# Attention's products with the probabilities and into the state as single float32 matmuls instead of three float16 ones

## The chip, the cores and the metric

The kernel runs on one core of a Trainium2 chip. The metric is the device time of one execution in microseconds (us), lower is better; runs are compared by their median. The engines are named as in the profile: PE is TensorE (matmul) and PEld its loads of the stationary operand, DVE is VectorE, ACT is ScalarE, POOL is GpSimd, SP is SyncE, which issues most DMAs.

## The reference

Three stages follow each other. An mLSTM attention over 4 batches, 8 heads, 768 tokens and 40 elements a head (a recurrence over tokens, with gates), a dense feed-forward layer of 3072 tokens (320 to 2048 to 320, leaky relu), and a layer of 8 experts (320 to 1024 to 320, relu) of which each token takes one:

```python
    for t in range(S):
        kt, vt, qt = (k[:, :, t], v[:, :, t], q[:, :, t])
        m_new = np.maximum(f_gate[:, :, t] + m, i_gate[:, :, t])
        f_stab = np.exp(f_gate[:, :, t] + m - m_new)
        i_stab = np.exp(i_gate[:, :, t] - m_new)
        m = m_new
        C = f_stab[:, :, None, None] * C + i_stab[:, :, None, None] * np.einsum('bhd,bhe->bhde', vt, kt)
        n = f_stab[:, :, None] * n + i_stab[:, :, None] * kt
        h_tilde = np.einsum('bhde,bhe->bhd', C, qt)
        nq = np.einsum('bhd,bhd->bh', n, qt)[:, :, None]
        denom = np.maximum(np.abs(nq), 1.0)
        y[:, :, t] = o * h_tilde / denom          # o: sigmoid of the output gate
...
    h = x @ w_in
    g = np.maximum(0.01 * h, h)
    return (g @ w_out).astype(np.float32)
...
    for e in range(E):
        mask = e_idx == e                         # e_idx: argmax of x @ w_gate
        h = np.maximum(x[mask] @ w1[e], 0.0)
        out[mask] = gate_w[mask, None] * eom[mask, e, None] * (h @ w2[e])
```

## The kernel before

**Attention** is computed in chunks of 128 tokens. A unit is one batch of one chunk with all 8 heads, so there are 24 units (6 chunks of 4 batches), each the function `unit`. Within a unit the scores are `k` times `q` (PE, line 762), DVE multiplies them by the decay between tokens (`gm`, line 366 as a helper), and the product, called probabilities here, is multiplied with the values, to which a column of ones is appended for the denominator (41 columns; PE, lines 782 to 784). What earlier chunks left comes from a state of 41 x 40 for each head (`o2`, line 799), and `state` (line 845 on) adds the weighted values of a chunk to it, for two batches at a time on two groups of output columns of PE (line 852). There are ten calls of `state`, two for each chunk but the last.

**Numbers.** Where a float32 operand enters a product, it is split into a float16 and a float16 remainder, and the product is three float16 products: high by high, high by low, low by high. The split is a scaled copy on ACT (`copy`, line 375) and a subtraction on DVE (`low`, line 363) or POOL (`less`, line 366). For the probabilities POOL also makes the float16 copy (line 768), but for the units in `PA`, where ACT does.

**Dense** work is 96 steps of two feed-forward tiles for a pair of 128-token tiles: 16 products in `gemm1` (line 903), leaky relu on ACT and DVE, a split by ACT and POOL (`gl`), then 12 products in `gemm2` (lines 925 to 927). The first steps need the attention of units 0 and 1 and the weights, which come as float64, are narrowed by integer operations on DVE and split. Behind the dense steps come the routing and 26 or more blocks of experts (lines 1169 to 1211).

**Order.** Every piece of work has a planned time (`UNITS`, `OFF`, `TICKS`, `WL`, ...). `Order.run` makes a list schedule of all instructions by planned time, with its own costs of operations (a float32 matmul at four times its columns), and writes out the order of each engine's queue. So on every engine an instruction that waits holds up all behind it. Buffers of attention are taken in turn from lists (`Bufs`): `raw_r` holds the loaded queries, keys and values, `QK` the split queries and keys, `GM` the decay and then the probabilities, `PH`/`PL`, `VH`/`VL` and `WVH`/`WVL` the split probabilities, values and weighted values. `S`, the PSUM tile of the scores, has one buffer, used by a unit's two halves of four heads in turn.

Of the kernel before, what the change touches and what calls it, by code (L numbers as in the profile page):

```python
# [25 lines left out]
E = 8  # L26
F = 1024
NTILE = NT // 128
PF = 10                      # pairs of tiles from here on share the dense weights' last pass
TA = 2 * PF                  # token tiles of the first dispatch  # L30
NBA = TA - E + 1             # full blocks that TA tiles always hold
NBH = E // 2                 # first blocks of the rest: up to half a block of two experts each
NBB = NBH + NTILE + E // 2 - 1 - NBA    # blocks of the rest, at most
# [3 lines left out]
S_V = 2.0 ** 5  # L37
S_C = 2.0 ** -4
S_N = 2.0 ** 15
# [25 lines left out]
class Slots:  # L65
    """a tile pool whose tags keep the order of their tiles"""
# [13 lines left out]
class Order:  # L80
    """the order of every engine's instructions: a list schedule by planned time"""
# [61 lines left out]
    def run(self, instrs, planned, pools):  # L143
# [49 lines left out]
        wait = {e: [] for e in self.ENGINES}     # (ready time, i)  # L193
        avail = {e: [] for e in self.ENGINES}    # (priority, i)
# [98 lines left out]
class Bufs:  # L293
    """buffers in turn, each free again once its last reader is out"""
# [12 lines left out]
# the plan: times of the units, of their stages, of the dense steps and of the weights' loads and splits  # L307
UNITS = [2.7, 0, 19, 17.2, 28.8, 32, 42.5, 46.5]
UNITS += [16 + 2.87 * i for i in range(16)]      # from the ninth on in ticks
# [20 lines left out]
# units whose decay between tokens the tensor engine adds up  # L330
PEU = 6
# what the Pool engine takes from the vector engine: packs, reciprocals times gates, gates from these chunks on,
# remainders of queries and keys, of weights
# [5 lines left out]
# units whose weights the scalar engine rounds; whose remainders the vector engine takes  # L339
PA = {3, 4, 6}  # L340
LV = {4}
# weights that the scalar engine scales; units with one transpose for query and key
WA = {(2, 0)}
MT = set()
# where blocks begin that few inputs use
RARE = [26, 28]
# the last planned time of a fixed order; lead and queue of the loads
# [5 lines left out]
def emit(tc, gates, qkv, og, w_in, w_out, w_gate, w1, w2, out):  # L353
# [23 lines left out]
    # arena views  # L377
# [44 lines left out]
    maskb = cp.tile([128, C], BF, name="maskb")      # -1e30 where the key is behind the query  # L422
# [47 lines left out]
    def narrow(r):  # L470
        """float64 words -> float32"""
        n = r.shape[1]
        cv = cv64()
        a, b = (x[:, 0:n] for x in cv)
        lo, hi = r[:, :, 0], r[:, :, 1]
        V.tensor_scalar(out=a, in0=hi, scalar1=3, scalar2=0x3FFFFFF8, op0=ALU.logical_shift_left,
                        op1=ALU.bitwise_and)
        yield 0.35
        stt(V, b, hi, -0x40000000, a, ALU.bitwise_and, ALU.bitwise_or)
        yield 0.65  # L480
        stt(V, a, lo, 29, b, ALU.logical_shift_right, ALU.bitwise_or)
        return a.bitcast(F32), cv

    def piece_win(j, blk, lead):
# [6 lines left out]
        if blk < 2:  # L491
            split(r, win_v[:, j, blk, :], win_v[:, j, 2 + blk, :], S_WIN, helper((j, blk)))
        else:
            # two column blocks' last rows: the remainders of each on the other half of the partitions
            for n in range(2):
                t, h, l = win_v[:, j + n, 4, :], slice(64 * n, 64 * n + 64), slice(64 - 64 * n, 128 - 64 * n)
                copy(t[h], r[h], S_WIN)
                low(t[l], r[h], S_WIN, t[h])
# [25 lines left out]
    def piece_w2(e, k0, n, until=0.0):  # L524
        """until: the time at which what lay there is used"""
# [24 lines left out]
    raw_r = Bufs([R.f32(2 * DM + H * D1) for _ in range(3)], "raw_r")  # L550
    QK = Bufs([R.f16(2, H, 128) for _ in range(4)], "QK")
    QKT = Bufs([R.f16(2 * H, 128) for _ in range(2)], "QKT")
    VH = Bufs([R.f16(H, 42) for _ in range(2)], "VH")
    VL = Bufs([R.f16(H, 42) for _ in range(2)], "VL")
    GM = Bufs([R.f32(H, C) for _ in range(3)], "GM")
    PH = Bufs([R.f16(4, C) for _ in range(4)], "PH")
    PL = Bufs([R.f16(4, C) for _ in range(4)], "PL")
    WV = Bufs([R.f32(H, D1) for _ in range(2)], "WV")
    WVH = Bufs([R.f16(H, 42) for _ in range(3)], "WVH")
    WVL = Bufs([R3.f16(H, 42) for _ in range(3)], "WVL")  # L560
# [26 lines left out]
    def parts(c):  # L587
        """g and b of chunk c as a sum of three bfloat16 parts, one on each group of 32 partitions"""
# [9 lines left out]
    def arguments(c, h0, tag):  # L598
        """g of the query + b of the key, masked, of four heads: [key, head, query]"""
# [15 lines left out]
    def emit_gates(c0, c1):  # L615
        """gates of chunks c0 to c1: g and b by token, decay of the chunk"""
# [33 lines left out]
        outs = [(gw, wT, S_V)]  # L650
# [19 lines left out]
    def emit_sig(c):  # L670
        """output gates of two chunks"""
# [15 lines left out]
    def unit(i):  # L687
        """one (batch, chunk) of all heads"""
# [18 lines left out]
        if i in QG:  # L707
            scaled(G, raw[:, 0:2 * DM], S_QK)
# [12 lines left out]
        else:  # L721
            for a, x in ((qt, qr), (kt, kr)):
                SP.dma_start_transpose(out=a, in_=x.rearrange("p h d -> p (h d)"))
        if i >= PEU:
# [15 lines left out]
        if c < NC - 1:  # L740
            wv, wvh, wvl = WV(), WVH(), WVL()
# [3 lines left out]
            yield 0.7  # L745
            copy(wvh[:, :, 0:D1], wv)
            yield 0.3
            less(True, wvl[:, :, 0:D1], wv, wvh[:, :, 0:D1])
            WV.free(wv)
            st[c, b] = (kr, wvh, wvl, qk)  # L750
        yield to("v")
        vh, vl = VH(), VL()
        copy(vh[:, :, 0:D1], v, S_V)
        low(vl[:, :, 0:D1], v, S_V, vh[:, :, 0:D1])
        raw_r.free(raw)
        pp = []
        for hf in range(2):
# [6 lines left out]
            ph, pl = PH(), PL()  # L764
            if i in PA:
                copy(ph, p32)
            else:
                G.tensor_scalar(out=ph, in0=p32, scalar1=1.0, scalar2=0.0, op0=ALU.mult, op1=ALU.add)
            yield 0.5
            less(not (i in LV), pl, p32, ph)  # L770
            if hf:
                GM.free(gm)
            pp.append((ph, pl))
# [4 lines left out]
        def pv(hf):  # L778
            ph, pl = pp[hf]
            for h in range(4):  # L780
                g = 4 * hf + h
                T.matmul(o1[:, g, :], ph[:, h, :], vh[:, g, 0:D1], start=True, stop=False)
                T.matmul(o1[:, g, :], ph[:, h, :], vl[:, g, 0:D1], start=False, stop=False)
                T.matmul(o1[:, g, :], pl[:, h, :], vh[:, g, 0:D1], start=False, stop=True)

        yield to("p")
        pv(0)
        pv(1)
        PH.free(pp[0][0], pp[1][0])
        PL.free(pp[0][1], pp[1][1])  # L790
        VH.free(vh)
        VL.free(vl)
# [36 lines left out]
        if c == NC - 1:  # L829
            QK.free(qk)  # L830
# [14 lines left out]
    def state(c, pr):  # L845
        up = ps.tile([128, H, D1], F32, tag="aux", name="up", bufs=3)
        for h in range(H):
            for m in range(3):
                for n, o in ((0, 0), (1, 64)):
                    kr, wvh, wvl, _ = st[c, 2 * pr + n]  # L850
                    k0, k1 = ((0, 64), (80, 128), (0, 64))[m] if n == 0 else ((0, 40), (80, 120), (0, 40))[m]
                    T.matmul(up[o:o + k1 - k0, h, :], kr[:, h, k0:k1], (wvh, wvh, wvl)[m][:, h, 0:D1],
                             start=(m == 0), stop=(m == 2))
        for n in range(2):
            QK.free(st[c, 2 * pr + n][3])
            WVH.free(st[c, 2 * pr + n][1])
            WVL.free(st[c, 2 * pr + n][2])
# [37 lines left out]
    def gemm1(xT, n, kp):  # L895
        """two feed-forward tiles: their leaky relu, split"""
# [54 lines left out]
    late = []           # for the logits of the last tiles, behind the first blocks of experts  # L951

# [1 line left out]
    def routing():  # L954
# [21 lines left out]
        half = [rt([128, E], F32, f"half{i}") for i in range(2)]      # block and row of an expert's half  # L976
# [12 lines left out]
        def dispatch(first, bufs, R1, RS, group):  # L989
            """slots of the blocks: their rows, tokens, scales and experts"""  # L990
# [23 lines left out]
            # scale  # L1014
# [9 lines left out]
            # rank in the expert  # L1024
# [22 lines left out]
            # blocks of the experts  # L1047
# [28 lines left out]
            # block of every token, out of the way for those that the other dispatch holds  # L1076
            def of_expert(i, a, r):
                """a of the expert of every token"""
# [8 lines left out]
            if not first:  # L1087
                # behind the full blocks: half a block
# [9 lines left out]
            # slot -> token  # L1098
# [23 lines left out]
            # row c * 512 + b * 128 + p is token b * 768 + c * 128 + p; none beyond the last  # L1122
# [52 lines left out]
        def experts(q):  # L1175
            """rows of the block and their expert: one for all or a fixed one for each half"""
# [42 lines left out]
        def chain(q0, q1, ahead):  # L1219
            """blocks q0 to q1, each one's second product after the next one's first"""  # L1220
# [105 lines left out]
    for j in range(4):  # L1326
        # these lie where the dense weights of steps up to t lay: two pieces of w_in, then w_out
# [76 lines left out]
```

## Time and profile before

| | before |
|---|---|
| median of 3 runs | 726.77 us (726.21 to 727.49) |
| span of the profiled execution | 721.0 us |
| PE busy | 596.5 us (83%), mean granted clock 0.966 |
| DVE busy | 486.8 us (68%) |
| ACT busy | 369.6 us (51%) |
| POOL busy | 391.2 us (54%) |

The span reaches from the first to the last instruction of the one execution that was profiled. That execution has no other time of its own; the median of the runs is 5.8 us above its span. PE's busy time is counted to modelled ends of overlapping matmuls, so distances between starts say more than durations. Shares over the whole span hide that the stages have different limits.

### The profile page before, as it was taken

To read this page: it belongs to the slowest core of one execution; us is meant where nothing else is said; L and a number is where in the kernel's file an instruction comes from. 1 tells how busy PE (TensorE), PEld (TensorE's weight loads), DVE (VectorE), ACT (ScalarE), POOL (GpSimd) and SP (SyncE) were. 2 spreads that over 40 slices of the span, in tenths; PEclk is the share of its full clock that TensorE was granted. 3 is DMA by queue.
4 is the path that set the end of the run, shared out by engine and by line. 5 is a ranking of instruction groups with operands and counts; after the bars stand their busy time and mean duration, and the time that the engine had idled before them with its cause. 6 is when DMAs were issued, how large, how long until landed. Compare 5 with 4: busy or idle time off the path is not lost. (4 is left out here: it accounts for less than half of the span.)

```text
span 721.0 us, 15741 instructions
## 1 busy us (share of the span) xinstructions
PE 596.5 (83%) x5624; PEld 426.0 (59%) x5624; DVE 486.8 (68%) x871; ACT 369.6 (51%) x772; POOL 391.2 (54%) x392
## 2 busy tenths in 40 slices
PE   3447779769787788977898899999699999999894
PEld 1235557547666566756676687776455655665552
DVE  7999999995588789779698876688635722122110
ACT  5546464677665676777655566655332222222220
POOL 6867887466866858867665544524523422223111
PEclk9997999999999999989999999999899999999997
DMA  8686893681957796987666656544599877777632
GB/s 226 228 150 85 184 259 111 209 215 27 186 159 159 211 237 123 228 185 178 136 161 153 170 153 193 155 129 129 165 198 180 160 155 131 159 151 154 148 88 50
DMA packets 215081, 116.77 MB, mean 162 GB/s; under 512 B 170011, under 2 KB 202523, under 8 KB 215004
## 3 DMA queue, kind: packets, MB, share of 16 engines
q1 hardware_dynamic: 212092, 106.68, 64.6%
q0 software_dynamic: 2912, 9.05, 4.5%
q8 instruction: 50, 0.82, 0.5%
q14 instruction: 27, 0.22, 0.1%
HBM read 64.58 MB, written 9.06 MB: 102 GB/s over the span
## 5 line engine op out<-in xcount | busy, mean ns | idle before, releaser
L903 PE MATMUL hp<-xT,arena 128*128 128x256 f16 x1536 | 197.2, 279 | 8.8 <-DVE g L366 7.8
L366 POOL TENSOR_TENSOR gl<-g,gh 128x512 f16<-128x512 f32 x96 | 131.8, 1374 | 111.1 <-ACT gh L375 108.7
L903 PEld LDWEIGHTS <-arena 128*128 128x128 f16 x1536 | 148.3, 100 | 31.5 <-issue 5.7
L925 PE MATMUL acc<-arena,gh 128*128 128x320 f16 x384 | 117.3, 307 | 14.3 <-DVE arena L1276 4.8
L927 PE MATMUL acc<-arena,gl 128*128 128x320 f16 x384 | 117.1, 308 | 9.9 <-POOL gl L366 9.8
L366 POOL TENSOR_TENSOR arena<-arena 128x512 f16<-128x512 f32 (+5 forms) x94 | 111.2, 1195 | 18.5 <-ACT arena L375 10.2
L926 PE MATMUL acc<-arena,gh 128*128 128x320 f16 x384 | 117.4, 306 | 0.5 <-POOL arena L366 0.5
L363 DVE SCALAR_TENSOR_TENSOR r<-hp,r 128x512 f16<-128x512 f32 x52 | 35.9, 691 | 120.8 <-ACT r L1194 106.5
L363 DVE SCALAR_TENSOR_TENSOR arena<-arena 128x328 f16<-128x328 f32 (+7 forms) x113 | 99.1, 888 | 9.3 <-ACT arena L375 7.1
L1188 PE MATMUL hp<-arena,xbb 128*128 (+1 forms) x480 | 95.5, 382 | 5.9 <-issue 5.6
L375 ACT ACTIVATE gh<-g 128x512 f16<-128x512 f32 x96 | 60.1, 626 | 70.3 <-DVE g L366 67.6
L366 DVE TENSOR_TENSOR g<-hp,t 128x512 f32<-128x512 f32 x96 | 65.2, 680 | 41.6 <-ACT t L375 36.0
L1207 PE MATMUL y<-arena,rT 128*128 (+1 forms) x720 | 90.4, 299 | 0.8 <-DMA rT<-r 0.5
L375 ACT ACTIVATE arena<-arena 128x328 f16<-128x328 f32 (+5 forms) x128 | 72.9, 599 | 33.3 <-DVE arena L363 12.7
L1207 PEld LDWEIGHTS <-rT 128*128 128x128 f16 (+1 forms) x720 | 61.8, 101 | 28.0 <-DMA rT<-r 1.4
L1211 POOL DMA_INDIRECT out<-ys,si x26 | 26.8, 1030 | 90.2 <-ACT ys L1210 83.3
L1188 PEld LDWEIGHTS <-xbb 128*128 128x128 f16 (+1 forms) x480 | 41.5, 102 | 53.1 <-issue 10.7
L375 ACT ACTIVATE t<-hp 128x512 f32<-128x512 f32 x96 | 56.1, 585 | 30.0 <-PE hp L903 29.9
L363 DVE SCALAR_TENSOR_TENSOR arena<-stg,arena 128x960 f16<-128x960 f32 (+3 forms) x48 | 57.5, 1198 | 15.3 <-ACT arena L375 14.9
L1194 ACT ACTIVATE r<-hp 128x512 f16<-128x512 f32 x52 | 31.0, 597 | 65.5 <-PE hp L1188 49.3
L375 ACT ACTIVATE arena<-stg 128x1024 f16<-128x1024 f32 (+2 forms) x48 | 46.9, 978 | 17.6 <-DMA stg<-w 10.6
L1169 POOL DMA_INDIRECT xbb<-x2rows,gi x26 | 28.0, 1077 | 49.0 <-PE hp L1188 42.9
(242 smaller groups left out, 855.3 us busy)
## 6 DMA issues: line engine op xcount, KB each, us to landing
stg<-w SPq DMA_DIRECT2D x24, 512.0 KB
arena<-qkv SPq DMA_DIRECT2D x24, 484.0 KB
arena<-gd SPq DMA_DIRECT2D x18, 512.0 KB
stg<-w SPq DMA_DIRECT2D x16, 480.0 KB
raw<-w_in SPq DMA_DIRECT2D x10, 512.0 KB
arena<-w_out SPq DMA_DIRECT2D x8, 640.0 KB
x2rows<-x2r SPq DMA_DIRECT2D x24, 192.0 KB
arena<-og SPq DMA_DIRECT2D x6, 640.0 KB
```

Of the source, the lines that this page charges most:

```text
L363: eng.scalar_tensor_tensor(out=o, in0=a, scalar=s, in1=b, op0=op0, op1=op1)
L366: eng.tensor_tensor(out=o, in0=a, in1=b, op=op)
L375: A.activation(out=o, in_=a, func=AF.Copy, scale=s)
L903: T.matmul(hp[:, kk, :], win_v[:, j, wb, o:o + 128], xT[:, xb, :], start=(m == 0), stop=(m == 7))
L925: T.matmul(acc[i], gh[:, kk, r], wh, start=(k == lo), stop=False)
L926: T.matmul(acc[i], gh[:, kk, r], wl, start=False, stop=False)
L927: T.matmul(acc[i], gl[:, kk, r], wh, start=False, stop=(k == hi))
L1169: G.indirect_dma_start(out=xb, out_offset=None, in_=rows, in_offset=bass.IndirectOffsetOnAxis(ap=gi[:, i:i + 1], axis=0), bounds_check=(TA ...
L1188: T.matmul(hp[n][r], xT[:, xb, r], W1v[:, e, wb, n * 512:(n + 1) * 512].rearrange("p a b -> p (a b)"), start=(m == 0), stop=(m == 7))
L1194: A.activation(out=r[:, 0, :], in_=hp[n], func=AF.Relu)
L1207: T.matmul(y[r], a[:, r], W2v[:, e, k, m, :].rearrange("p a b -> p (a b)"), start=(k + n == 0), stop=(k == 7 and n == 2))
L1211: G.indirect_dma_start(out=out, out_offset=bass.IndirectOffsetOnAxis(ap=D_[s][1][:, i:i + 1], axis=0), in_=ys, in_offset=None, bounds_chec ...
```

## The change

The products of probabilities and values, and those of keys and weighted values into the state, take the float32 operands as they are: one float32 matmul in place of three float16 ones. The splits of probabilities, values and weighted values go, with their buffers. In their place there are more buffers for what is now held longer: six of `raw_r` (the state reads keys from it, so it is freed only there), four of `GM` and of `WV`, and two instead of four of `QK`, freed behind the transposes. Where POOL scales queries and keys, it writes to a buffer of its own (`QKS`) and no longer in place, since the state needs the unscaled keys. The constants of scale follow. The plan's times are unchanged. Comments, which the change also removes, are left out here:

```diff
-S_V = 2.0 ** 5
-S_C = 2.0 ** -4
-S_N = 2.0 ** 15
+S_W = 2.0 ** 5
+S_C = 2.0
+S_N = S_QK * S_QK
...
-PA = {3, 4, 6}
-LV = {4}
...
-    raw_r = Bufs([R.f32(2 * DM + H * D1) for _ in range(3)], "raw_r")
-    QK = Bufs([R.f16(2, H, 128) for _ in range(4)], "QK")
+    raw_r = Bufs([R.f32(2 * DM + H * D1) for _ in range(6)], "raw_r")
+    QKS = R.f32(2 * DM)
+    QK = Bufs([R.f16(2, H, 128) for _ in range(2)], "QK")
     QKT = Bufs([R.f16(2 * H, 128) for _ in range(2)], "QKT")
-    VH = Bufs([R.f16(H, 42) for _ in range(2)], "VH")
-    VL = Bufs([R.f16(H, 42) for _ in range(2)], "VL")
-    GM = Bufs([R.f32(H, C) for _ in range(3)], "GM")
-    PH = Bufs([R.f16(4, C) for _ in range(4)], "PH")
-    PL = Bufs([R.f16(4, C) for _ in range(4)], "PL")
-    WV = Bufs([R.f32(H, D1) for _ in range(2)], "WV")
-    WVH = Bufs([R.f16(H, 42) for _ in range(3)], "WVH")
-    WVL = Bufs([R3.f16(H, 42) for _ in range(3)], "WVL")
+    GM = Bufs([R.f32(H, C) for _ in range(4)], "GM")
+    WV = Bufs([R.f32(H, D1) for _ in range(4)], "WV")
...
         if i in QG:
-            scaled(G, raw[:, 0:2 * DM], S_QK)
+            G.tensor_scalar(out=QKS, in0=raw[:, 0:2 * DM], scalar1=S_QK, scalar2=0.0, op0=ALU.mult, op1=ALU.add)
+            q, k = (QKS[:, u * DM:(u + 1) * DM].rearrange("p (h d) -> p h d", h=H) for u in range(2))
...
             for a, x in ((qt, qr), (kt, kr)):
                 SP.dma_start_transpose(out=a, in_=x.rearrange("p h d -> p (h d)"))
+        QK.free(qk)
...
         if c < NC - 1:
-            wv, wvh, wvl = WV(), WVH(), WVL()
+            wv = WV()
             w = wT[:, c, b * H:(b + 1) * H].unsqueeze(2)
             tt(G, wv, v, w.to_broadcast([128, H, D1]), ALU.mult)
-            yield 0.7
-            copy(wvh[:, :, 0:D1], wv)
-            yield 0.3
-            less(True, wvl[:, :, 0:D1], wv, wvh[:, :, 0:D1])
-            WV.free(wv)
-            st[c, b] = (kr, wvh, wvl, qk)
-        yield to("v")
-        vh, vl = VH(), VL()
-        copy(vh[:, :, 0:D1], v, S_V)
-        low(vl[:, :, 0:D1], v, S_V, vh[:, :, 0:D1])
-        raw_r.free(raw)
-        pp = []
+            st[c, b] = (raw, wv)
         for hf in range(2):
...
             tt(V, p32, sc, p32, ALU.mult)
-            ph, pl = PH(), PL()
-            if i in PA:
-                copy(ph, p32)
-            else:
-                G.tensor_scalar(out=ph, in0=p32, scalar1=1.0, scalar2=0.0, op0=ALU.mult, op1=ALU.add)
-            yield 0.5
-            less(not (i in LV), pl, p32, ph)
-            if hf:
-                GM.free(gm)
-            pp.append((ph, pl))
...
-        def pv(hf):
-            ph, pl = pp[hf]
-            for h in range(4):
-                g = 4 * hf + h
-                T.matmul(o1[:, g, :], ph[:, h, :], vh[:, g, 0:D1], start=True, stop=False)
-                T.matmul(o1[:, g, :], ph[:, h, :], vl[:, g, 0:D1], start=False, stop=False)
-                T.matmul(o1[:, g, :], pl[:, h, :], vh[:, g, 0:D1], start=False, stop=True)
-
         yield to("p")
-        pv(0)
-        pv(1)
...
+        for h in range(H):
+            T.matmul(o1[:, h, :], gm[:, h, :], v[:, h, :], start=True, stop=True)
+        GM.free(gm)
+        if c == NC - 1:
+            raw_r.free(raw)
...
         for h in range(H):
-            for m in range(3):
-                for n, o in ((0, 0), (1, 64)):
-                    kr, wvh, wvl, _ = st[c, 2 * pr + n]
-                    k0, k1 = ((0, 64), (80, 128), (0, 64))[m] if n == 0 else ((0, 40), (80, 120), (0, 40))[m]
-                    T.matmul(up[o:o + k1 - k0, h, :], kr[:, h, k0:k1], (wvh, wvh, wvl)[m][:, h, 0:D1],
-                             start=(m == 0), stop=(m == 2))
+            for n, o in ((0, 0), (1, 64)):
+                raw, wv = st[c, 2 * pr + n]
+                k0 = DM + h * D
+                T.matmul(up[o:o + 64 - 24 * n, h, :], raw[:, k0:k0 + 64 - 24 * n], wv[:, h, :], start=True, stop=True)
         for n in range(2):
-            QK.free(st[c, 2 * pr + n][3])
-            WVH.free(st[c, 2 * pr + n][1])
-            WVL.free(st[c, 2 * pr + n][2])
+            raw_r.free(st[c, 2 * pr + n][0])
+            WV.free(st[c, 2 * pr + n][1])
```

## Rows read from the trace of the kernel before

**Rows 1.** Busy time by stage: stretch, length, busy us (instructions) of each engine, clock.

```profile
0.00:48.00 48.00, 18.60 (x165) 11.04 (x166) 43.04 (x69) 27.54 (x54) 35.22 (x65) 1.00 0.81 215
48.00:160.00 112.00, 84.67 (x900) 63.82 (x901) 107.34 (x159) 63.20 (x135) 79.25 (x68) 0.92 0.74 173
160.00:410.00 250.00, 208.60 (x2414) 164.88 (x2414) 199.17 (x330) 167.63 (x386) 173.90 (x164) 0.97 0.70 164
410.00:510.00 100.00, 96.79 (x851) 76.74 (x850) 74.59 (x140) 59.36 (x101) 42.70 (x36) 1.00 0.54 153
```

(The engines are PE, PEld, DVE, ACT and POOL in this order; behind the clock stand the share of DMA and GB/s.)

**Rows 2.** Timeline of PE, two dense steps: start us, length, line, operands, count.

```profile
446.56 1.91 PE L903 MATMUL hp<-xT,arena 128*128 128x256 f16 x16
449.94 1.91 PE L903 MATMUL hp<-xT,arena 128*128 128x256 f16 x16
```

**Rows 3.** PE's waits from 160 to 410 us: total us, times, longest.

```profile
PE sc L762 <- DVE arena L366: 16.4, 10, 4.0
...
PE o L784 <- POOL arena L366: 6.0, 7, 1.8
PE acc L925 <- DVE arena L1276: 3.9, 1, 3.9
PE acc L925 <- DVE arena L366: 3.8, 3, 1.9
PE hp L903 <- DVE g L366: 2.4, 1, 2.4
PE o L782 <- POOL arena L768: 1.7, 3, 0.6
```

**Rows 4.** Groups of instructions on POOL, whole span: count, busy us, mean ns.

```profile
L366 POOL TENSOR_TENSOR arena<-arena 128x512 f16<-128x512 f32 x48 | 63.9, 1337 | 2.7 <-ACT arena L375 1.1
L768 POOL TENSOR_SCALAR arena<-arena 128x512 f16<-128x512 f32 x42 | 30.4, 724 | 15.3 <-DVE arena L366 14.5 <-DVE rd L366 0.7
...
L366 POOL TENSOR_TENSOR arena<-arena 128x328 f16<-128x328 f32 x20 | 20.2, 1017 | 6.0 <-ACT arena L375 5.8
```

**Rows 5.** The same on DVE, from 0 to 160 us.

```profile
L363 DVE SCALAR_TENSOR_TENSOR arena<-arena 128x328 f16<-128x328 f32 x9 | 7.0, 776 | 0.2
...
L366 DVE TENSOR_TENSOR arena<-arena 128x512 f16<-128x512 f32 x2 | 1.5, 734 | 0.0
```

**Rows 6.** The same on DVE, whole span: one operation with its input elsewhere.

```profile
L363 DVE SCALAR_TENSOR_TENSOR x2r<-arena,x2r 128x256 f16<-128x256 f32 x20 | 14.5, 725 | 0.7 <-ACT x2r L375 0.6
...
L363 DVE SCALAR_TENSOR_TENSOR x2r<-acc,x2r 128x256 f16<-128x256 f32 x4 | 1.7, 417 | 0.4 <-ACT x2r L375 0.4
```

(`arena` lies in SBUF, `acc` in PSUM.)

**Rows 7.** Busy time of line 363 alone: stretch, length, DVE us, clock, DMA.

```profile
0.00:160.00 160.00, 83.78 (x99) 0.95 0.76 185
160.00:410.00 250.00, 107.35 (x136) 0.97 0.70 164
```

**Rows 8.** Timeline of PE: first and last of twelve value products in a row.

```profile
69.12 0.18 PE L784 MATMUL o<-arena 128*128 128x41 f16 x1
...
69.40 0.18 PE L783 MATMUL o<-arena 128*128 128x41 f16 x1
```

**Rows 9.** Timeline of PE: float32 transposes and the product behind them.

```profile
67.47 0.43 PE L661 MATMUL pt<-ident,arena 32*128 32x32 f32 x4
67.83 0.31 PE L927 MATMUL acc<-arena,gl 128*128 128x320 f16 x1
```

**Rows 10.** Weight loads, float32 and float16: least, median and greatest ns.

```profile
L661 PEld LDWEIGHTS pt<-ident,arena x16: 133/138/219, 7.2 to 70.5; 32*128 32x128 f32 x16
...
L782 PEld LDWEIGHTS <-arena x192: 95/96/152, 21.7 to 405.4; 128*128 128x128 f16 x192
```

**Rows 11.** Timeline of PE: one state of 48 products and what follows.

```profile
240.59 0.89 PE L852 MATMUL up<-arena 128*64 128x41 f16 x48
241.40 0.28 PE L903 MATMUL hp<-xT,arena 128*128 128x256 f16 x1
```

**Rows 12.** Busy time of line 782 alone (a third of the value products).

```profile
160.00:410.00 250.00, 12.55 (x128) 10.54 (x128) 0.97 0.70 164
```

More of the change, by code (lines that the diff above doesn't have):

```diff
@@ L649, in emit_gates @@
         yield GW
-        outs = [(gw, wT, S_V)]
+        outs = [(gw, wT, S_W)]
         if c0:
@@ L776, in unit @@
         o1 = ps.tile([128, H, D1], F32, tag="aux", name="o1", bufs=3)
-        def pv(hf):
-            ph, pl = pp[hf]
-            for h in range(4):
-                g = 4 * hf + h
-                T.matmul(o1[:, g, :], ph[:, h, :], vh[:, g, 0:D1], start=True, stop=False)
-                T.matmul(o1[:, g, :], ph[:, h, :], vl[:, g, 0:D1], start=False, stop=False)
-                T.matmul(o1[:, g, :], pl[:, h, :], vh[:, g, 0:D1], start=False, stop=True)
-        yield to("p")
-        pv(0)
-        pv(1)
[L789 to L792, printed above, removed]
+        yield to("p")
+        for h in range(H):
[3 more added lines that the diff above has]
+            raw_r.free(raw)
         yield to("c")
@@ L828, in unit @@
         SP.dma_start_transpose(out=xTs[i // 2][:, :, j * 128:(j + 1) * 128], in_=xr)
-        if c == NC - 1:
-            QK.free(qk)
         if c < NC - 1 and b % 2:
```

## Prediction

> **What bounds the kernel now.** I read the busy table by stage first [rows 1]. Up to 48 us there are only the first attention units, the gates and the conversion of the weights; the dense steps start there. Up to 160 us VectorE (DVE) is busy 43.0 of 48 us and then 107.3 of 112 us, so it is the bound; TensorE (PE) has 27 us of idle time in the second of these stretches. From 160 to 410 us nothing is full: PE 208.6 of 250 us, DVE 199.2, GpSimd (POOL) 173.9, ScalarE (ACT) 167.6. From 410 to 510 us, with attention over, PE is busy 96.8 of 100 us. What follows (some 211 us of expert blocks) holds no line that the change touches. Dense steps at full pace follow each other by 3.38 us [rows 2]; 96 of them are 324 us of the 462 us between 48 and 510, and the rest is attention's own PE work and PE idle time. So the end moves by PE's idle time and PE's work up to 510 us, whichever engine causes it. In the third stretch I read who ends PE's idle time [rows 3]: the scores wait for DVE 16.4 us (one PSUM buffer for both halves of a unit, so the second half's scores wait until DVE has multiplied the first), the dense products wait for DVE 3.9, 3.8 and 2.4 us, and the value products wait for POOL, which splits the probabilities, 6.0 and 1.7 us. This gives 26.5 us behind DVE's queue and 7.7 us behind the split itself; most of what is left of the idle time waits on a transpose by DMA that nothing here touches.
>
> **What is taken away.** Off POOL go the rounding of probabilities (42 x 724 ns = 30.4 us), their remainders (46 of the 48 of that shape, the other two split weights: 46 x 1.337 = 61.5 us) and the remainders of weighted values (20.2 us), 112 us in all [rows 4]. Off ACT go 44 copies of 328 elements and six of 512. Off DVE go 24 remainders of values; nine of them, 7.0 us, lie before 160 us, and the two of probabilities, 1.5 us, too [rows 5]. The value products' wait for POOL is gone; next in line for them is DVE's multiply of the second half, which ends before the split did, so I count the 7.7 us as gained.
>
> **What a lighter POOL gives DVE.** The same remainder of 256 elements takes 725 ns with both operands in SBUF and 417 ns with one in PSUM [rows 6]: 42% of the former is lost to something that the latter doesn't meet, and POOL, busy for most of both stretches, is the other engine that works on SBUF in this way. Remainders and other such operations of that line are 83.8 us of DVE before 160 us and 107.4 us from 160 to 410 [rows 7]. Before 160 us: 83.8 - 7.0 = 76.8 us, 42% of it 32 us. POOL is busy 35.2 + 79.3 = 114.5 us there [rows 1] and loses the work of units 0 to 7, 10 x 0.724 + 14 x 1.337 + 8 x 1.017 = 34 us, 30%. So the gain lies between 0 and 32 x 0.30 = 9.6 us; nothing shows which of the two engines' operations overlap, and I take the middle, 5 us.
>
> **The stretch before 160 us.** DVE sets its length, so it shortens by 7.0 + 1.5 + 5 = 13.5 us (ends: 8.5 and 18.1; below the lower end only if DMA, at 0.74 to 0.81 of its engines' time [rows 1], comes to bind).
>
> **The stretch from 160 to 410 us.** DVE loses 15 remainders, some 12 us at the mean of [rows 5], and by the same reckoning between 0 and 18 us of contention: (107.4 - 12) x 0.42 = 40 us, of which POOL loses (32 x 0.724 + 32 x 1.337 + 12 x 1.017) / 173.9 = 45%. With the middle, 9 us, its busy share falls from 199/250 = 0.80 to 178/250 = 0.71. Time spent behind a queue goes about as u/(1 - u), 3.9 before and 2.5 after, so 37% of the 26.5 us goes: 9.8 us (ends: 0 and 26.5). With the 7.7 us this is 17.5 us of PE idle time.
>
> **What is added: float32 products.** No row of before shows one. 24 f16 products of a unit start about 25.5 ns apart [rows 8], 0.61 us a unit. Now there are 8 in float32. The nearest rows are float32 transposes with 128 stationary columns, on 32 partitions and moving only 32 columns: four take 0.43 us with the last one's length of 0.222, so they start 69 ns apart, and the next f16 product starts 0.36 us after the first, 90 ns for each [rows 9]. Their weight loads last 138 ns by the median, f16's of 128 columns 96 [rows 10]. Lower end: 70 ns, a transpose's price. Upper end: 4 x 69 = 276 ns, if each float32 product costs four such passes with their loads. I take the geometric middle, 140 ns. The state is now 16 float32 products in place of 48 f16 ones, which took 240.59 to 241.40 us, 17 ns each, since two column groups run side by side [rows 11]; I keep that ratio of 17/25.5 for float32. With x us for a product, units 8 to 23 (16 of them: 128 products of each kind after 160 us, 8 a unit [rows 12]) and the six states of chunks 2 to 4 add 16 (8x - 0.61) + 6 (16 * 0.667x - 0.81) = 192x - 14.7 us: at 140 ns 12.2 us; at 70 ns -1.3; at 276 ns 38.3. I count all of it, since PE becomes the bound of this stretch. For units 0 to 7 it is 8 * 0.51 + 4 * 0.68 = 6.8 us and hides in PE's 27 us of idle time before 160 us; without that cover it would be on the path too.
>
> The float32 weight load is where pages speak against this change. The Trainium skill, page "TensorE: Matmul & The Clock Gate", section "Weight-path perf modes", says that the fast weight load is off for FP32; the 138 ns against 96 [rows 10] agree in direction. The page "FP8 and Floating Point Precision", section "TensorE Precision Notes", says that true FP32 makes four passes through the array; no row here shows one. With four passes at the f16 row's 25.5 ns, an estimate from that page, x would be 102 ns and the sum 7.3 us lower than mine; with four passes that each reload at 69 ns it would be the upper end.
>
> **What I cost at nothing.** The scaled queries and keys go to one separate buffer (eight units): the same operation on POOL, and its wait for the unit before, whose readers are ACT's two copies and POOL's own remainders, is covered by the distance between units, 250/16 = 15.6 us after 160 us. If that cover fails, gates and weighted values queue behind it on POOL, about a microsecond each. QK falls from four to two buffers, but is free after the transposes rather than after the state; if they are late, ACT's copy of the unit after next waits, and dense copies behind it. Inputs are held until the state, in six buffers instead of three: if one isn't free, the load waits on SP's queue, and the transposes and weight loads behind it. The gate buffers are four now for a longer hold. All are in proportion to the longer or shorter holds.
>
> **Sum.** Before 160 us -13.5; after -17.5 + 12.2 = -5.3; together -18.8 us. The profiled span is 721.0 us, the median of the runs 726.77, so 5.8 us lie around the span. 721.0 - 18.8 + 5.8 = 708 us.
>
> **Rivals.**
> - *Float32 is dear* (the other side). PE pays 276 ns a product; the relief is the same 13.5 + 17.5 = 31 us, the price 38.3: +7.3, 734 us. The change loses from 192x - 14.7 = 31, x = 238 ns. For it: PE is 83% busy in that stretch, and the loads of float32 are slower in the rows. Against it: the transposes' 69 to 90 ns. By itself: the page on precision, with its four passes, is the rule that would make it so.
> - *Float32 is cheap.* 70 ns: -31 - 1.3, 694 us. For it: the transposes' spacing; against it: they move fewer columns and only pass on what they read.
> - *The relief is not passed on.* The order on each engine is written out, so a freed POOL or DVE may only wait elsewhere: no gain from contention or from DVE's queue. -8.5 - 7.7 + 12.2 = -4.0, 723 us. For it: after 160 us no engine is full; against it: the waits of [rows 3] are short and many, behind a queue.
> - *The buffers bind*, or an order that the planner writes anew stalls somewhere: of unknown size, both signs, 10 us or so.
>
> **How the numbers follow.** About the forecast (700 to 717) 0.42; cheap float32 or more relief (below 700) 0.20; relief not passed on (717 to 729) 0.20; dear float32 (above) 0.15; buffers and order 0.03. Within 0.2% of 726.8, about what a measurement of this kernel can tell from no change, is 725.3 to 728.2. Faster: 0.42 + 0.20 + most of the third, 0.13 = 0.75; slower 0.18; same 0.07. The range from 688 to 733 leaves out the deep end of the second case and most of the fourth.
>
> **What would show it.** Right: 108 instructions fewer on POOL, 26 on DVE, 50 on ACT, 704 on PE; value products that start about 140 ns apart; DVE's SBUF remainders well below 725 ns; scores waiting less for DVE; the dense steps ending near 490 us instead of 510 and the same 211 us after it. Wrong: value products at 240 ns or more; DVE's operations no shorter; a new wait on inputs or on the two QK buffers at ACT or SP; or the DVE-bound stretch no shorter than 150 us.

## The result, and the profile after

The changed kernel takes 703.36 us (median of 4 runs, 700.39 to 704.15), the kernel before 727.13 us in the same comparison (4 runs): a ratio of 0.966, with a 95% interval from 0.9636 to 0.9684. The prediction was 708 us. The execution that was profiled took 700.39 us, its span is 698.6 us. Of the kernels further down, one execution in four with doubled products and four in ten with POOL's work back lay more than 1.5% above the fastest of the same kernel; medians are of the others.

Busy time and instructions of the changed kernel's whole span:

```profile
span 698.6 us, 14850 instructions
PE 620.8 (89%) x5272; PEld 461.1 (66%) x5272; DVE 435.7 (62%) x845; ACT 350.5 (50%) x722; POOL 275.4 (39%) x282
```

POOL lost 115.8 us, DVE 51.1, ACT 19.1, and PE gained 24.3. By stage, with the columns of [rows 1]:

```profile
0.00:48.00 48.00, 28.08 (x163) 20.12 (x164) 35.75 (x70) 24.70 (x46) 21.48 (x51) 1.00 0.81 214
48.00:160.00 112.00, 96.53 (x854) 78.03 (x852) 94.66 (x151) 65.59 (x137) 63.34 (x52) 0.91 0.71 181
160.00:410.00 250.00, 234.49 (x2310) 193.89 (x2308) 180.01 (x328) 161.10 (x362) 100.31 (x93) 0.98 0.73 173
410.00:510.00 100.00, 87.41 (x714) 65.86 (x713) 71.03 (x145) 53.43 (x95) 38.06 (x33) 0.97 0.58 153
```

From 160 to 410 us PE is now busy 234.5 of 250 us, where it was 208.6; DVE is no longer full in the first two stretches (35.8 of 48 and 94.7 of 112 us). PE has become the bound behind 160 us. Its waits there, to be read beside [rows 3]:

```profile
PE lp L908 <- DMA x2T<-x2r: 7.2, 8, 2.3
PE sc L745 <- DVE arena L363: 6.5, 6, 2.0
PE lp L908 <- DVE rd L363: 1.4, 1, 1.4
PE acc L887 <- POOL gl L363: 0.3, 1, 0.3
```

The value products wait for nobody any more (7.7 us before), the dense products no longer for DVE (10.1 us before), the scores 6.5 us in place of 16.4. Where the time went is seen in the products of `gemm1` (first start to last start, us), line 903 before and 863 after:

```profile
L903 PE MATMUL hp<-xT,arena x1536: 269/273/422, 48.7 to 510.4; 128*128 128x256 f16 x192
```

```profile
L863 PE MATMUL hp<-xT,arena x1536: 269/273/421, 43.4 to 491.3; 128*128 128x256 f16 x192
```

The dense steps start 5.3 us and end 19.1 us earlier; from that end on it is 207.3 us where it was 210.6.

The new products, grouped (those of probabilities and values, then the state's, for each of its two groups of columns) and on PE's timeline:

```profile
L753 PE MATMUL o<-arena 128*128 128x41 f32 x384 | 52.7, 300 | 0.0
...
L814 PE MATMUL up<-arena 128*64 128x41 f32 x160 | 13.1, 247 | 0.0
L814 PE MATMUL up<-arena 128*40 128x41 f32 x160 | 11.3, 227 | 0.0
```

```profile
200.20 1.13 PE L814 MATMUL up<-arena 128*64 128x41 f32 x32
201.25 1.92 PE L863 MATMUL hp<-xT,arena 128*128 128x256 f16 x16
...
204.64 1.88 PE L753 MATMUL o<-arena 128*128 128x41 f32 x16
206.34 0.37 PE L763 MATMUL o<-arena 120*128 120x41 f16 x8
```

There are 384 instructions for 192 products and 320 for 160: each float32 product is two passes, with a weight load each. A unit's 16 passes take 1.70 us to the start of what follows, 106 ns a pass, 212 ns a product, where three f16 products took 0.61 us a unit [rows 8]; the state's 32 passes take 1.05 us, 66 ns a product, where f16 took 0.81 [rows 11].

### The profile page after: what moved, and what is told of

It reads as the page before. It is cut to its first block, busy times and chain, and to the rows that moved or that the text cites. A ratio compares the mean times of both kernels' runs of the same rounds, so it can differ in the third digit from the quotient of the medians.

```text
span 698.6 us, 14850 instructions
## 1 busy us (share of the span) xinstructions
PE 620.8 (89%) x5272; PEld 461.1 (66%) x5272; DVE 435.7 (62%) x845; ACT 350.5 (50%) x722; POOL 275.4 (39%) x282
## 5 line engine op out<-in xcount | busy, mean ns | idle before, releaser
L363 POOL TENSOR_TENSOR gl<-g,gh 128x512 f16<-128x512 f32 x96 | 125.4, 1307 | 198.2 <-ACT gh L372 186.5
L863 PE MATMUL hp<-xT,arena 128*128 128x256 f16 x1536 | 191.6, 277 | 9.7 <-DVE g L363 5.9
L887 PE MATMUL acc<-arena,gl 128*128 128x320 f16 x384 | 115.5, 305 | 6.1 <-POOL gl L363 6.1
L360 DVE SCALAR_TENSOR_TENSOR arena<-arena 128x320 f16<-128x320 f32 (+6 forms) x89 | 69.1, 785 | 12.3 <-ACT arena L372 11.8
L372 ACT ACTIVATE arena<-arena 128x640 f16<-128x640 f32 (+3 forms) x78 | 50.9, 672 | 26.2 <-DVE arena L360 7.6
L1171 POOL DMA_INDIRECT out<-ys,si x26 | 26.5, 1018 | 88.3 <-ACT ys L1170 80.5
L730 ACT ACTIVATE arena<-arena,bT 128x128 f32<-128x128 f32 x144 | 48.2, 389 | 9.5 <-POOL arena L719 9.4
L753 PE MATMUL o<-arena 128*128 128x41 f32 x384 | 52.7, 300 | 0.0
```

The source lines that it names most:

```text
L360: eng.scalar_tensor_tensor(out=o, in0=a, scalar=s, in1=b, op0=op0, op1=op1)
L363: eng.tensor_tensor(out=o, in0=a, in1=b, op=op)
L372: A.activation(out=o, in_=a, func=AF.Copy, scale=s)
L730: A.activation(out=gm[:, 4 * hf + h, :], in_=gm[:, 4 * hf + h, :], func=AF.Exp, bias=bT[:, c, g:g + 1])
L753: T.matmul(o1[:, h, :], gm[:, h, :], v[:, h, :], start=True, stop=True)
L863: T.matmul(hp[:, kk, :], win_v[:, j, wb, o:o + 128], xT[:, xb, :], start=(m == 0), stop=(m == 7))
```

## The experiments

Theory A is that of the prediction: lifting the splits off POOL, DVE and ACT frees PE from waiting, and PE pays the price of float32 in full where it has become the bound. Rival B: what counted was the products' own wait for the split, and PE hides the price. Rival C came up on the way: the time is a matter of the order that the planner happens to write.

Ratios below are to the kernel before on the same chip, with 95% intervals; differences in us are between medians, to the 703.4 us of the changed kernel unless said otherwise.

**The price on PE, doubled.**

```diff
         for h in range(H):
-            T.matmul(o1[:, h, :], gm[:, h, :], v[:, h, :], start=True, stop=True)
+            for _ in range(2):
+                T.matmul(o1[:, h, :], gm[:, h, :], v[:, h, :], start=True, stop=True)
```

> The changed kernel, but each of the 8 float32 products of probabilities and values is issued twice (the second overwrites the first with the same numbers), so PE gets a second 1.70 us a unit, 41 us in all, and no other engine anything. Theory A (PE is the bound after 150 us, so its price is paid in full there): 16 of 24 units pay, +27 us, and up to 8 us more from the first eight: 728 to 738 us. Rival B (PE still has idle time in which products hide; what the change won was the wait for the split itself): at most half of the 41 us shows, 710 to 720 us.

Measured: 754.2 us, ratio 1.0333 (1.0258 to 1.0408), 51 us more. B is out, and more came than even the 41 us of extra work. Where the rest lies is shown by the timeline of two units' doubled products and by the busy time of the stage:

```profile
203.20 3.66 PE L754 MATMUL o<-arena 128*128 128x41 f32 x32
206.69 1.48 PE L864 MATMUL hp<-xT,arena 128*128 128x256 f16 x12
...
236.73 5.87 PE L754 MATMUL o<-arena 128*128 128x41 f32 x32
242.40 0.48 PE L764 MATMUL o<-arena 120*128 120x41 f16 x8
```

```profile
160.00:410.00 250.00, 237.56 (x2198) 198.50 (x2198) 147.91 (x283) 144.63 (x330) 89.22 (x84) 0.92 0.62 145
```

The granted clock is 0.92 in this stage (mean of 2.4 GHz and stretches at 1.2), 0.98 without the doubling. The same products take 3.5 us at 203 and 5.7 us at 237 us, and from 240 to 280 us the clock is 0.81. Of the first eight units, whose price the prediction had as hidden, the first two take 6.8 us each in place of 3.5, and the dense steps start at 48.1 us in place of 43.4: there it isn't hidden either. These passes take some 212 ns each, with the products doubled as without, twice the 106 ns of later ones; the rows show a granted clock of 1.00 up to 48 us, so they don't say why.

**The price on PE, taken away.**

```diff
+    def top(a):
+        return a.bitcast(BF).rearrange("p (d w) -> p d w", w=2)[:, :, 1]
...
-            T.matmul(o1[:, h, :], gm[:, h, :], v[:, h, :], start=True, stop=True)
+            T.matmul(o1[:, h, :], top(gm[:, h, :]), top(v[:, h, :]), start=True, stop=True)
```

> The changed kernel, but the products of probabilities and values read only the upper 16 bits of each float32 number, as one bfloat16 product: no engine but PE does anything else, the numbers are coarser (left out: the lower 16 bits). PE loses about 1.70 - 0.2 = 1.5 us a unit if the pitch of 25.5 ns of a float16 product holds. Theory A: 16 x 1.5 = 24 us less, 675 to 683 us. Rival B: PE's price is hidden, 693 to 703 us.

Measured: 685.2 us, ratio 0.9436 (0.9369 to 0.9502), 18 us less; A said 20 to 28, B 0 to 10. The eight products of a unit take 0.20 us to the next start, as the expectation had it:

```profile
199.44 0.36 PE L756 MATMUL o<-arena 128*128 128x41 bf16 x8
199.64 0.36 PE L766 MATMUL o<-arena 120*128 120x41 f16 x8
```

So most of the price that PE pays for float32 here is in the end time. At the head it is hidden: the dense steps start at 44.3 us here, no earlier than the 43.4 us of the changed kernel. For this kernel, as for the other variants, the planner writes the order anew; what that alone is worth comes further down.

**The work of the split back on POOL, for nobody.** The results go to a scratch tile (`DH`, `DW`) and the float32 products stay.

```diff
+PA = {3, 4, 6}
+LV = {4}
...
+    DH, DV, DW = R3.f16(4, C), R3.f16(H, 42)[:, :, 0:D1], R3.f16(H, 42)[:, :, 0:D1]
+    for t in (DH, DV, DW):
+        G.memset(t, 0.0)
...
             tt(G, wv, v, w.to_broadcast([128, H, D1]), ALU.mult)
+            yield 0.7
+            pass
+            yield 0.3
+            less(True, DW, wv, DW)
...
             tt(V, p32, sc, p32, ALU.mult)
+            ph = pl = DH
+            if i not in PA:
+                G.tensor_scalar(out=ph, in0=p32, scalar1=1.0, scalar2=0.0, op0=ALU.mult, op1=ALU.add)
+            yield 0.5
+            if i not in LV:
+                less(True, pl, p32, ph)
```

> The changed kernel, but POOL again does its work of the split (42 copies and 46 differences of 512 elements, 20 differences of 328, about 112 us) into a scratch tile that nobody reads: no product waits for it. Theory A (a lighter POOL relieves DVE and POOL's own queue): DVE's difference x2r<-arena of 256 elements goes back from 606 towards 725 ns, and the time rises by 10 to 20 us, 714 to 724 us. Rival B (only the products' own wait for the split counted): at most +5 us, 703 to 708 us, with x2r at about 606 ns.

Measured: 714.7 us, ratio 0.9847 (0.9799 to 0.9895), 11 us more: within A's range, near its lower end, and above B's. Busy time (of an execution of 722.6 us):

```profile
PE 625.5 (87%) x5272; PEld 461.7 (64%) x5272; DVE 470.9 (65%) x845; ACT 350.3 (49%) x722; POOL 395.4 (55%) x393
```

DVE has the same 845 instructions as the changed kernel and takes 470.9 us for them instead of 435.7: 120 us of POOL's work cost DVE 35 us. The one row that I had named as a sign, the difference of 256 elements, went from 606 only to 662 ns; it turned out to wander between 525 and 716 ns from one order to the next in kernels whose DVE and POOL do the same work, so it says nothing, and DVE's total does.

PE's waits from 160 to 410 us, to be read beside [rows 3]:

```profile
PE lp L923 <- DMA x2T<-x2r: 13.8, 11, 2.2
PE sc L754 <- DVE arena L365: 6.1, 4, 2.3
PE hp L878 <- DVE g L365: 1.2, 1, 1.2
PE acc L900 <- DVE arena L1260: 0.8, 1, 0.8
```

Behind DVE's queue PE waits 8.1 us, hardly more than the 6.5 us of the changed kernel and far from the 26.5 us of before, although DVE is busy 192.6 of the 250 us here (199.2 before, 180.0 in the changed kernel).

**The work of the split back on all three engines.** As before, and also ACT's copies, DVE's remainders of the values (`low(DV, v, 32.0, DV)`) and the two of probabilities, all into scratch.

> The changed kernel, but POOL, DVE and ACT all do their work of the split again, into scratch that nobody reads; the products stay float32 and wait for none of it. Theory A: the kernel before, less the products' wait for the split (7.7 us) and plus the price of float32 on PE (18.9 us after 150 us), so 733 to 743 us, slower than before. Rival B: 705 to 712 us.

Measured: 738.4 us, ratio 1.0131 (1.0077 to 1.0186): 35 us above the changed kernel, and slower than before, as A said.

```profile
PE 634.1 (86%) x5272; PEld 465.9 (63%) x5272; DVE 485.1 (66%) x871; ACT 369.1 (50%) x772; POOL 390.0 (53%) x393
```

The engines but PE are busy as before (DVE 486.8, ACT 369.6, POOL 391.2 us there). Without the splits' removal the change is a loss, and since this kernel has all buffers of the changed one, those alone bring no gain. From before to this kernel two things differ by design: PE pays for float32, 16 x (1.70 - 0.61) + 6 x (1.05 - 0.81) = 18.9 us behind 160 us, and the value products no longer wait for the split, 7.7 us [rows 3]. That makes +11.2 us; measured are +11.6 (the interval is 5.6 to 13.5). That the two agree so closely is luck: the order is new too, each scratch tile is one buffer where the splits had two to four, and PE's waits behind DVE's queue from 160 to 410 us are 16.4 us here, not the 26.5 us of before.

**What sets the price of a pass.** Two sets of products with fewer columns in front of the real ones; the results are overwritten.

```diff
         for h in range(H):
+            T.matmul(o1[:, h, 0:20], gm[:, h, :], v[:, h, 0:20], start=True, stop=True)
+        for h in range(H):
+            T.matmul(o1[0:64, h, :], gm[:, h, 0:64], v[:, h, :], start=True, stop=True)
+        for h in range(H):
             T.matmul(o1[:, h, :], gm[:, h, :], v[:, h, :], start=True, stop=True)
```

> The changed kernel with two further sets of 8 float32 products in front of the real ones of each unit, whose results are overwritten: one moves 20 columns in place of 41, one holds 64 stationary columns in place of 128. If loading the stationary operand sets the price of 106 ns a pass, the first set keeps 106 ns and the second falls to about 66 ns or less (the state's passes of 64 and 40 columns start 33 ns apart, two groups side by side). If the moved columns set it, the first set falls to about 52 ns and the second keeps 106 ns. The whole time is of no interest here (some 45 to 60 us above the changed kernel).

```profile
252.34 1.86 PE L753 MATMUL o<-arena 128*128 128x20 f32 x16
254.13 1.13 PE L755 MATMUL o<-arena 128*64 128x41 f32 x16
255.19 2.48 PE L757 MATMUL o<-arena 128*128 128x41 f32 x16
```

With 20 moved columns 16 passes take 1.79 us to the next start, no less than 41 columns take (1.70). With 64 stationary columns they take 1.06 us, 66 ns a pass. So at these sizes the stationary operand sets the price, and with 128 stationary columns the count of moved ones doesn't. It isn't the columns of the load alone: the float32 transposes of before also hold 128, on 32 partitions, and start 69 to 90 ns apart [rows 9]; what makes that difference no run shows. The kernel took 790.9 us in its one execution, 88 us above the changed kernel where 45 to 60 were expected; its granted clock was 0.931 over the span. The Trainium skill, page "TensorE: Matmul & The Clock Gate", section "LDWEIGHTS (loading the stationary operand)", gives the time of a load in nanoseconds as the columns divided by 1.2. Estimated from that, 128 columns are 106.7 ns and 64 columns 53 ns: the distance of passes agrees for 128 (106) and not for 64 (66).

**Half of the change.** Float32 for the probabilities only; the state's three f16 products come back, with their copies and differences, `raw_r` at 4 and `QK` at 4 buffers.

> Half of the change: the products of probabilities and values are float32, those into the state are the three float16 ones again, with ACT's copy and POOL's difference of the weighted values (20 each, 9.3 and 20.2 us), and the buffers that go with it (four of inputs, four of QK). Theory A: POOL's share of the gain in proportion, 20.2/112 of the 19.6 us of all POOL work, 3.5 us, 1 us for ACT, less 2 us that PE saves: 704 to 709 us. Rival (the buffers of the change, held to the state, cost something, or the state's part is where the gain lies): below 700 or above 712 us.

Measured: 710.0 us, ratio 0.976 (0.9708 to 0.9813). It is 6.6 us above the changed kernel and just outside what A gave, which took POOL's whole work at 19.6 us (by the run above it is 11 us). By what the next two runs show, this doesn't tell the two halves apart: the difference is no larger than what order alone makes. Since 710.0 us is 14 us or more below every order of before (see below), it does show that the larger part of the gain needs only the probabilities, and not the buffers held until the state.

**Order alone.** The planner's cost of every float32 instruction on PE, and the planned distance of the dense steps; no instruction is added or taken away.

```diff
-            n *= 4 if mybir.dt.size(q.ins[0].bass_ap.dtype) == 4 else 1
+            n *= 12 if mybir.dt.size(q.ins[0].bass_ap.dtype) == 4 else 1
```

```diff
-TICK = 3.38
+TICK = 3.36
```

> The changed kernel, but its planner takes a float32 product of 41 columns for 205 ns, about what it takes on the chip (212 ns), in place of 68 ns; the instructions are the same, only their order on the engines is written anew. Theory A: nothing in sight depends on it, within 4 us of the changed kernel, 699 to 707 us. Rival C (the gain is a matter of a lucky order): 10 us or more away.

> The changed kernel with the planned distance of dense steps at 3.36 in place of 3.38: no work changes, only the order that the planner writes. It shows how much of any difference between two kernels here is a matter of order. Theory A: within 4 us, 699 to 707 us. Rival C: 10 us or more away.

Measured: with the higher price in the planner 721.2 us (ratio 0.9919, 0.9892 to 0.9946), with 3.36 713.5 us (0.9802, 0.976 to 0.9844). Rival C is right at least so far: order alone is worth 10 to 18 us here. The higher price is right only for the products with the values (205 ns, 212 measured): a product of the state gets 205 ns too, where it takes 66, and a transpose of 32 columns 160 ns, where it takes 69 to 90 [rows 9]. With it, PE's idle time from 40 to 500 us is this:

```profile
PE lp L908 <- DMA x2T<-x2r: 16.4, 13, 3.6
PE sc L745 <- DVE arena L363: 13.4, 5, 4.2
PE hp L863 <- DMA xT<-xr: 8.1, 2, 5.5
```

In the changed kernel the first two are 8.9 and 8.1 us, and the third doesn't occur among its waits. DVE, ACT and POOL are hardly busier or less (425.2, 352.0 and 276.7 us). So I asked how much of the 24 us is order.

**Orders of before, and more of after.** `TICK` at 3.36 and 3.40 in the kernel before, at 3.40 and 3.34 in the changed one.

> The kernel before with the planned distance of dense steps at 3.36 in place of 3.38: no work changes, only the written order. The changed kernel moved from 703 to 714 us by the same edit, so order is worth some 10 us there. Theory A (the change is worth 20 us or so, whatever the order): 720 to 738 us, above all orders of the changed kernel. Rival C (much of the difference is a lucky order of the changed kernel, or an unlucky one of before): 705 to 715 us.

> The kernel before with 3.40: a third order of the same work. Theory A: 720 to 738 us. Rival C: 705 to 715 us.

> The changed kernel with 3.40. Theory A: 700 to 716 us, the mean of its orders some 18 us below that of before. Rival C: 715 to 725 us.

> The changed kernel with 3.34. Theory A: 700 to 716 us. Rival C: 715 to 725 us.

| TICK | before, us | changed, us | ratio of changed |
|---|---|---|---|
| 3.34 | | 705.2 | 0.9721 (0.9682 to 0.9759) |
| 3.36 | 724.4 | 713.5 | 0.9802 (0.976 to 0.9844) |
| 3.38 (as given) | 726.5 | 703.4 | 0.966 (0.9636 to 0.9684) |
| 3.40 | 725.2 | 711.7 | 0.9795 (0.9751 to 0.9839) |
| mean | 725.4 | 708.5 | |

(Ratios are each from the run's own comparison; 3.34 was not run for the kernel before.) The orders of before lie within 2 us of each other, those of the changed kernel within 10 (18 with the other price). Every order of the changed kernel is below every order of before. The change is worth about 17 us by these means (14 with the 721.2 us among its orders), and the order that it happened to get another 5. Against the mean of 708.5 us, the runs above read +46 (products doubled), -23 (products cheap), +6 (POOL's work back) and +30 (all work back); the first, second and last are outside all orders seen, that of POOL alone is not, so its 6 to 11 us may be order, while DVE's 35 us are not: DVE's busy time lies between 425 and 436 us in all five orders of the changed kernel.

No version tried here that does the whole work is faster than the changed kernel as it stands.

## Why the prediction held, step by step

- **The sum** was 708 us: 5 us above the kernel as given, and within 1 us of the mean of its four orders. That is better than its terms deserve: the price of float32 was 7 us too low, the gain before 160 us 6 us too high and the relief behind it 8.5 us too low, and that they nearly cancel is luck. Of the 19.1 us by which the dense steps end earlier some 4 us are in none of these terms, nor are the 3.3 us behind the dense steps, where the prediction had no change.
- **The price of float32** was the geometric middle, 140 ns; it is 212 ns for probabilities and values and 66 instead of 93 ns for the state. Behind 160 us it is 18.9 us in place of 12.2. The step that failed is the choice of a middle between a transpose's 70 ns and four times 69: [rows 9] are one pass, and a product here is two passes of 106 ns, each of them dearer than a transpose (the loads last 192 ns by the median, those of the transposes 138). The doubled instructions show in the counts: PE lost 352 instructions, not the 704 that I named; those of DVE and ACT fell by 26 and 50, as said, POOL's by 110 (108 said).
- **That PE pays in full behind 160 us** holds, within what order leaves open, by the runs with doubled and cheap products (+46 to +51 us for 41 us of work, -18 to -23 where 24 were due). **That the first eight units hide theirs** failed in the doubled run: the first two stand at the head of everything, and their passes take twice as long as later ones. In the changed kernel this is covered: the dense steps start 5.3 us earlier than before, and no earlier still with the cheap products.
- **The relief behind 160 us** was mis-sized low: 7.7 us for the wait on the split and 37% of 26.5 us behind DVE's queue. The first went entirely, of the second 20.0 us are gone (26.5 to 6.5). PE's idle time fell from 41.4 to 15.5 us, 26 us where I had 17.5. The share by u/(1 - u) was not only too timid: with POOL's work back DVE's busy share is 0.77, which by that rule leaves 23 of the 26.5 us, and PE waits 8.1 us. So, as far as this one order shows, this part of the gain did not come by a lighter POOL making DVE less busy; with all three engines' work back the wait is 16.4 us. Which of the removed operations, or how much of order, shortened it stays open.
- **The contention between POOL and DVE** was the right mechanism, and of line 363 about the right size. The same line (360 after), to be read beside [rows 7]:

```profile
0.00:160.00 160.00, 69.35 (x92) 0.94 0.74 191
160.00:410.00 250.00, 85.30 (x125) 0.98 0.73 173
```

  It lost 83.8 + 107.4 - 69.4 - 85.3 = 36.5 us, of which the 24 remainders were 24 x 0.776 = 18.6 at the price of [rows 5]; the other 18 us are mostly operations that became shorter, where the prediction had 5 + 9. I had left out DVE's other lines: over all of DVE it is 51.1 us less, 18.6 + 1.5 of them removed work, so 31 us. The run with POOL's work back gives DVE 35 us again, which shows it directly; what it is worth in the end time is not clear of order.
- **The stretch before 160 us** was to shorten by 13.5 us. The 19th group of 16 products of `gemm1` (289 to 304) starts at 154.57 us before and at 146.99 us in the changed kernel (first its row of before, then of after): 7.6 us, less than the lower end of 8.5.

```profile
154.57 1.91 PE L903 MATMUL hp<-xT,arena 128*128 128x256 f16 x16 [0.68 <-DVE g L366]
146.99 1.91 PE L863 MATMUL hp<-xT,arena 128*128 128x256 f16 x16
```

- **What was costed at nothing** did not all stay so. No new wait on inputs, `QK` or the scaled copy stands among PE's from 160 to 410 us, but the prediction's own sign was a wait at ACT or SP, and there is one. Up to 510 us ACT's copies wait for the transposes that free `QK`:

```profile
ACT arena L372 <- DMA arena<-arena: 5.9, 5, 1.6
```

  In no order of the kernel before does this wait occur, nor in half of the change, with four buffers of `QK`; in the other orders of the changed kernel it is 6.5 to 9.6 us. SP's loads of the gates (line 691) wait 18.1 us for PE to read the buffer before, where the kernel before (line 699) had 5.4 us for POOL. Whether these waits cost time was not tried.
- **What lies around the span** was a small error: I took 5.8 us as the distance of median and span. Of the changed kernel's profiled execution it is 700.39 - 698.6 = 1.8 us, and 1.7 to 1.9 us in every later execution of the kernel before (up to 2.2 us with POOL's work back). So the execution profiled before was some 4 us faster than the median; its own time isn't known.
- **The rival of a dear float32** had its break-even at 238 ns with the relief of 31 us. The price came close to it, 212 ns; it didn't decide because the relief was larger (38 us: the 19 us that the dense steps end earlier plus the 18.9 that PE pays).
- **Not foreseen** was how far order alone moves the changed kernel. I gave "an order that stalls somewhere" 0.03 and 10 us; five orders of it span 703 to 721 us. With PE at 94% behind 160 us, there may be less slack to take up a transpose that is late by a few us, but why the planner with the higher price writes the worst order is not settled: the rows show that its PE waits more for transposes and scores, and its ACT longest for `QK` (9.6 us), not why.

## What to carry to other kernels

A split that saves time on PE is paid on three other engines; when PE has idle time because it waits for them, dearer products on PE can be a gain, as here, until PE is the bound, and then most of what is further added on PE is in the end time. Count work taken off one engine together with what it gives to the engine that works on the same memory beside it: DVE's total at the same instruction count shows it, single rows don't. And where a planner writes the order, compare a few orders of both kernels before a difference of one or two per cent is put down to the change.

## What the runs showed of the hardware

- A float32 product is two passes with a weight load each; a pass costs 106 ns with 128 stationary columns and 41 moved ones (16 of them 1.70 us), 112 ns with 20 moved ones (1.79 us), and 66 ns with 64 stationary and 41 moved (1.06 us). Two column groups of 64 and 40 columns ran side by side at 33 ns a pass.
- 120 us more of POOL's work on SBUF made DVE's unchanged 845 instructions 35 us longer (435.7 to 470.9 us).
- With 32 float32 passes in a row for each unit, the granted clock of the profiled execution was 0.92 from 160 to 410 us, against 0.98 with 16. It fell while the engine did such passes (the 32 from 236.7 us took 5.7 us; 0.81 from 240 to 280 us), but the same number of them at 203.2 us ran at the full clock to the end (3.5 us).
